# 64-bit weights narrowed to float32 by instructions on 1024 columns instead of 512

## The chip, the cores and the metric

The kernel runs on one core of a Trainium2 chip. The metric is the device time of one execution in microseconds. The engines are PE (matrix products; PEld is its weight load), DVE (vector), ACT (activation), POOL (GpSimd) and SP, which here only starts transfers. Each engine works through its own instructions in a fixed order and waits on semaphores that the others raise.

## The reference

Memory attention feeds a gated layer, whose output feeds eight experts, of which each token uses two:

```python
a = exp(phi - max(phi, axis=seq)); a = a / sum(a, axis=seq)          # 4 x 8 heads, 576 tokens, 32 slots
k_m, v_m = einsum(a, k), einsum(a, v)
attn = softmax(0.125 * q @ k_m.T) ;  x = attn @ v_m                  # x: 2304 x 512
h = x @ moe_w_in ;  x = (h * sigmoid(h)) @ moe_w_out                 # 512 x 2048, 2048 x 512
top2 of (x @ w_gate + log1p(exp(x @ w_noise)) * noise), softmax over the two
out[tokens of e] += weight * (relu(x @ w1[e]) @ w2[e])               # 8 experts, 512 x 1024 x 512
```

`moe_w_in` and `moe_w_out` are arrays of 64-bit floats, so the kernel sees each of their elements as two 32-bit integers, the low word and the high word.

## The kernel before

The span falls into four batches of attention and gated layer and then the experts. All products are made of float32 values split into a high part and a low part (`hi`, `lo`, each rounded for PE), so that three products stand for one.

**The gated layer.** A batch has 16 blocks `f` of 128 hidden columns and two token pieces `i` (256 and 320 tokens), which makes 32 steps `s`. Step `s` calls `mlp_h` (six products into the PSUM tile `h`, of which there are two; ACT makes `th`, DVE multiplies it, ACT and DVE or POOL split it into `gh` and `gl`), and three steps later `mlp_x` multiplies `gh`, `gl` by `woh[f]` and `wol[f]` (L299 to L301), into four PSUM tiles that stay open over the batch. A table of hooks (`at(step, function, ...)`) puts everything else at a step. A scheduler then fixes each engine's order.

**The weights.** In batch 0 alone the 64-bit weights are narrowed to float32 on the way. `moe_w_in` comes in eight parts of 256 columns (1 MB each, loaded as two halves of 512 element pairs a partition), is narrowed into `wi` (L237 to L238), is stored to `win_d` for the later batches, and is multiplied into the attention's values by `project` (L146), whose output is split into `wph`, `wpl`. `moe_w_out` comes in sixteen parts of 512 KB, one for each `f`. Narrowing one part of 512 columns is: ACT scales the low word to three bits (`lw`, L200), ACT scales the high word (L201), DVE shifts and joins them (L206); then for `w_in` DVE writes the sign (L210), and for `w_out` ACT takes the sign (`cg`, L216), POOL multiplies by it (L221), ACT makes `woh` (L264), and DVE (even `f`) or POOL (odd `f`) makes `wol` (L265). The loads go into the tag `st`, four buffers of 4 KB a partition; later the same buffers hold small tiles of the routing (`xs`, `xt`, `lt`, `z`, `xa`, `w1s`).

**The start.** The first instructions are written by hand after the loads: the softmax of batch 0 in two token pieces, `project(0, 1)`, the first `mlp_h`, then `narrow_wout(0)`, `narrow_win(1)` and `project(1, 1)` at step 2.

## Time and profile before

| what | us |
|---|---|
| median of three runs (lowest, highest) | 895.47 (894.5, 896.85) |
| the profiled execution, its own time | 896.81 |
| its span, first to last instruction | 895.0 |
| PE busy in the span | 847.6 (95%) |
| DVE, ACT, POOL busy in the span | 474.2, 359.2, 230.8 |
| PE busy in the first 45 us | 25.0 |

The span is what the profile covers; 1.8 us of the execution lie around it. Busy time of PE counts matmuls whose ends are modelled and which overlap, so it says where PE has work and not how fast it does it. An idle stretch is put down to what ended it.

### The profile page before, as it was taken

What the parts mean: (1) busy time and instruction counts of PE and PEld (TensorE: products, weight loads), DVE (VectorE), ACT (ScalarE), POOL (GpSimd) and SP (SyncE); (2) the same over time, 40 slices, a digit from 0 to 9 for tenths busy, and PEclk for the clock granted to TensorE, in tenths of its full rate; (3) what the DMA queues carried; (4) which work ended last, traced back from release to release, by engine and by line L of the source; (5) the groups of instructions that cost most, each with busy time, mean ns of one, the idle gap of its engine ahead of it and who ended that gap; (6) DMA issues with size and microseconds to landing.
All of it is one profiled execution on the core that took longest, in us unless ns stands there. A gap on an engine that the chain in (4) does not pass through costs nothing. (4 is left out here: it accounts for less than half of the span.)

```text
span 895.0 us, 14479 instructions
## 1 busy us (share of the span) xinstructions
PE 847.6 (95%) x5524; PEld 711.0 (79%) x5524; DVE 474.2 (53%) x1133; ACT 359.2 (40%) x836; POOL 230.8 (26%) x231
## 2 busy tenths in 40 slices
PE   4699899999999899999899999999999999999995
PEld 2367577788787787887889989989889798897983
DVE  3898995785277556554635444334444344343411
ACT  2689875444234354452214333324333133231400
POOL 0244340002000400310453234034342443322311
PEclk8599999999999999999999999999999999999998
DMA  9899842533201146221446455254552655424311
GB/s 306 273 323 330 267 154 94 168 130 65 86 5 48 48 158 243 57 75 49 106 145 197 151 167 170 62 177 135 149 144 72 188 148 158 132 80 138 88 26 38
DMA packets 76054, 124.14 MB, mean 139 GB/s; under 512 B 27715, under 2 KB 39363, under 8 KB 75975
## 3 DMA queue, kind: packets, MB, share of 16 engines
q1 hardware_dynamic: 46199, 90.66, 31.5%
q0 software_dynamic: 29776, 32.46, 12.7%
q8 instruction: 45, 0.74, 0.4%
q14 instruction: 34, 0.28, 0.1%
HBM read 99.69 MB, written 23.81 MB: 138 GB/s over the span
## 5 line engine op out<-in xcount | busy, mean ns | idle before, releaser
L597 PE MATMUL x<-w,gh 128*128 128x512 f32 (+5 forms) x640 | 202.5, 397 | 0.0
L597 PEld LDWEIGHTS x<-w,gh 128*128 128x128 f32 (+5 forms) x640 | 114.3, 183 | 27.5
L597 PE MATMUL x<-w,gl 128*128 128x512 f32 (+5 forms) x320 | 125.7, 393 | 0.0
L581 PE MATMUL x<-xh,w 128*128 128x290 f32 (+7 forms) x512 | 119.5, 306 | 0.0
L581 PE MATMUL h<-xh,w 128*128 128x290 f32 (+7 forms) x512 | 118.0, 303 | 1.0 <-issue 1.0
L277 PE MATMUL h<-ah,wph 128*128 128x320 f32 (+1 forms) x512 | 112.0, 303 | 2.5 <-DVE th L282 1.3
L299 PE MATMUL x<-woh,gh 128*128 128x512 f32 x256 | 106.7, 419 | 0.4 <-ACT woh L264 0.2
L277 PEld LDWEIGHTS h<-ah,wph 128*128 128x128 f32 x512 | 89.9, 192 | 19.0 <-DVE th L282 4.3
L300 PE MATMUL x<-wol,gh 128*128 128x512 f32 x256 | 102.3, 400 | 1.9 <-POOL wol L265 1.9
L301 PE MATMUL x<-woh,gl 128*128 128x512 f32 x256 | 101.5, 397 | 0.8 <-DVE gl L286 0.7
L444 POOL DMA_INDIRECT tab_d<-rows,slot x36 | 35.6, 988 | 240.3 <-DVE slot L441 192.2
L581 PEld LDWEIGHTS x<-xh,w 128*128 128x128 f32 x512 | 88.4, 190 | 0.0
L581 PEld LDWEIGHTS h<-xh,w 128*128 128x128 f32 x512 | 87.3, 189 | 1.0 <-issue 0.6
L282 DVE SCALAR_TENSOR_TENSOR th<-th,h 128x256 f32<-128x256 f32 (+1 forms) x128 | 57.6, 450 | 56.1 <-ACT th L280 43.2
L280 ACT ACTIVATE th<-h 128x256 f32<-128x256 f32 (+1 forms) x128 | 52.1, 407 | 82.9 <-PE h L277 66.6
L607 DVE SCALAR_TENSOR_TENSOR y<-x,tab,ex 116x512 f32<-116x512 f32 (+5 forms) x35 | 26.3, 750 | 109.6 <-PE x L597 105.3
L543 POOL DMA_INDIRECT xg<-x_d,gid x37 | 46.4, 1255 | 145.3 <-PE aux L563 76.6
L581 PE MATMUL h<-xl,w 128*128 128x290 f32 (+7 forms) x256 | 77.6, 303 | 1.1 <-issue 1.1
L581 PE MATMUL x<-xl,w 128*128 128x290 f32 (+7 forms) x256 | 78.6, 307 | 0.0
L277 PE MATMUL h<-ah,wpl 128*128 128x256 f32 (+1 forms) x256 | 76.4, 298 | 0.0
L285 ACT ACTIVATE gh<-th 128x256 fp32r<-128x256 f32 x128 | 53.2, 416 | 53.9 <-DVE th L282 49.3
L610 POOL DMA_INDIRECT out<-y,tab x40 | 51.7, 1292 | 87.6 <-DVE y L607 81.0
(167 smaller groups left out, 1391.8 us busy)
## 6 DMA issues: line engine op xcount, KB each, us to landing
w1s<-moe_w SPq DMA_DIRECT2D x32, 512.0 KB
w2s<-moe_w SPq DMA_DIRECT2D x32, 512.0 KB
wi<-win_d SPq DMA_DIRECT2D x24, 512.0 KB
kv<-kv SPq DMA_DIRECT2D x16, 650.0 KB
st<-moe_w_in SPq DMA_DIRECT2D x16, 512.0 KB
st<-moe_w_out SPq DMA_DIRECT2D x16, 512.0 KB
q<-qt SPq DMA_DIRECT2D x16, 288.0 KB
out<-z SPq DMA_DIRECT2D x1, 4608.0 KB
```

What stands on the lines that cost most here:

```text
L277: pe.matmul(p[:, :w], wt[:, g, c:c + 128], AH[b, g][at][:, t0:t0 + w], start=(n == 0), stop=(n == 5))
L280: act.activation(th[:, :w], p[:, :w], AF.Tanh, scale=0.5)
L282: dve.scalar_tensor_tensor(u[:, :w], th[:, :w], 1.0, p[:, :w], op0=OP.add, op1=OP.mult)
L285: act.activation(gh, u[:, :256], AF.Copy)
L299: pe.matmul(X2[j], gh[:, r], woh[f], start=(f == 0), stop=False)
L300: pe.matmul(X2[j], gh[:, r], wol[f], start=False, stop=False)
L301: pe.matmul(X2[j], gl[:, r], woh[f], start=False, stop=(f == NF - 1))
L444: st = pool.indirect_dma_start(out=tab_d, out_offset=bass.IndirectOffsetOnAxis(ap=slot[:, j, k:k + 1], axis=0), in_=rows.bitcast(I32)[:, j ...
L543: last = pool.indirect_dma_start(out=XG[k, j], out_offset=None, in_=x2_d if k else x2_d[:KNOWN, :], in_offset=bass.IndirectOffsetOnAxis(ap ...
L581: pe.matmul(p[:, :w], wt[:, d, c], x[:, d, r], start=(n == 0), stop=(n == 11))
L597: mm = pe.matmul(p, g[:, r], w[:, f, :], start=(n == 0), stop=(n == 23))
L610: st = pool.indirect_dma_start(out=a["out"], out_offset=bass.IndirectOffsetOnAxis(ap=TAB[k][:, j, 0:1], axis=0), in_=y, in_offset=None, bo ...
```

## The change

Three things change in the code. The low words are written back in place, into the loaded buffer, so the tile `lw` is gone. The loads go into a pool of their own with three buffers of 8 KB a partition, each filled by two loads (`raw`), and all of the narrowing but that of part 0 of `w_in` and of parts 0 and 1 of `w_out` is done by instructions on 1024 columns: a part of `w_in` at once, and the parts of `w_out` in pairs, fetched at step 2f-6 and narrowed at step 2f-2. A pair has one `wo` tile (before: two tiles in turn, one part each), and POOL makes the low parts of every second pair, DVE those of the others. At step 32 the pool is closed and a pool with the tag `st` (four buffers) is opened in its place for the routing's small tiles. [...]

```diff
-    def stage(src):
-        t = m1.tile([128, 512, 2], I32, name="st", tag="st", bufs=4)
-        sp.dma_start(t.rearrange("p a w -> p (a w)").rearrange("p (c x) -> p c x", c=src.shape[1]), src)
+    def stage(src, x=0, t=None):
+        t = t or s0.tile([128, 1024, 2], I32, name="raw", bufs=3)
+        v = t[:, 512 * x:512 * (x + 1), :].rearrange("p a w -> p (a w)")
+        sp.dma_start(v.rearrange("p (c x) -> p c x", c=src.shape[1]), src)
         return t
 
     def shrink(t, m):
-        low = ap_.tile([128, 512], I32, name="lw", bufs=1)
-        act.activation(low, t[:, :, 0].bitcast(U32), AF.Identity, scale=LOW, bias=lowb)
+        low = t[:, :, 0]
+        act.activation(low, low.bitcast(U32), AF.Identity, scale=LOW, bias=lowb)
...
-            g = ap_.tile([128, 512], BF16, name="cg", bufs=1)
+            g = ap_.tile([128, 1024], BF16, name="cg", bufs=1)[:, :t.shape[1]]
...
-        for g, t in enumerate(ST.pop(("i", i))):
-            narrow(t, WI[i][:, 2 * g:2 * g + 2, :].rearrange("p r f -> p (r f)"), True)
+        narrow(ST.pop(("i", i)), WI[i].rearrange("p r f -> p (r f)"), True)
...
-    def narrow_wout(i):
-        w = ap_.tile([128, DM], F32, name="wo", bufs=2)
-        narrow(ST.pop(("o", i)), w)
-        act.activation(woh[i], w, AF.Copy)
-        (pool if i % 2 else dve).tensor_sub(wol[i], w, woh[i].bitcast(F32))
+    def narrow_wout(i, n=2):
+        t = ST["o", i // 2]
+        r = slice(i % 2 * DM, (i % 2 + n) * DM)
+        hi, lo = (x[i // 2][:, r] for x in wop)
+        w = ap_.tile([128, 2 * DM], F32, name="wo", bufs=1)[:, :n * DM]
+        narrow(t[:, r, :], w)
+        act.activation(hi, w, AF.Copy)
+        (pool if i // 2 % 2 else dve).tensor_sub(lo, w, hi.bitcast(F32))
...
-    for f in range(1, NF):
-        at(max(0, 2 * f - 5), fetch_wout, f)
-        at(2 * f - 1, narrow_wout, f)
+    at(0, fetch_wout, 1)
+    at(1, narrow_wout, 1, 1)
+    for f in range(2, NF, 2):
+        for x in range(2):
+            at(max(0, 2 * f - 6), fetch_wout, f + x)
+        at(2 * f - 2, narrow_wout, f)
...
+    at(32, open_s1)
...
-    nc = bacc.Bacc("TRN2", target_bir_lowering=False, num_devices=1)
+    nc = bacc.Bacc("TRN2", target_bir_lowering=False, num_devices=1,
+                   dynamic_dma_scratch_size=8192)
```

The orders of the engines differ in batch 0 alone; from PE's instruction 336 on (of some 4370 rows) they are the same. Three places follow.

**The first narrowings, on ACT and DVE.** These are ACT's instructions from the first narrowing of `w_out` (`wo`, `cg`, `woh`) to the first `th`, before:

```order
L200 ACTIVATE lw<-st,lowb 128x512
L201 ACTIVATE wo<-st 128x512
L216 ACTIVATE cg<-st 128x512
L201 ACTIVATE wi<-st 128x512
L200 ACTIVATE lw<-st,lowb 128x512
L264 ACTIVATE woh_89<-wo 128x512
L201 ACTIVATE wi<-st 128x512
L163 ACTIVATE sct<-sct 128x2x320
L200 ACTIVATE lw<-st,lowb 128x512
L280 ACTIVATE th<-h 128x256
```

And the same stretch in the change:

```order
L204 ACTIVATE raw<-raw,lowb 128x512
L205 ACTIVATE wo<-raw 128x512
L220 ACTIVATE cg<-raw 128x512
L204 ACTIVATE raw<-raw,lowb 128x1024
L271 ACTIVATE woh_92<-wo 128x512
L166 ACTIVATE sct<-sct 128x2x320
L205 ACTIVATE wi<-raw 128x1024
L287 ACTIVATE th<-h 128x256
```

The copy of the high words of `w_in` part 1 stood half before and half behind `woh`; now it stands as a whole behind `woh` and the softmax's exponential (L163, now L166). DVE's rows there, from the softmax's second token piece (`smx` is its maximum, `ssm` its sum) to the sign of `w_in` part 1, are these in the change:

```order
L164 TENSOR_REDUCE smx<-sct 128x2x10
L210 SCALAR_TENSOR_TENSOR wo<-wo,raw 128x512
L165 TENSOR_TENSOR sct<-sct,smx 128x2x320
L272 TENSOR_TENSOR wol_100<-wo,woh_92 128x512
L173 TENSOR_REDUCE ssm<-sct 128x2x10
L174 TENSOR_SCALAR ssm<-ssm 128x2x10
L210 SCALAR_TENSOR_TENSOR wi<-wi,raw 128x1024
L175 RECIPROCAL ssm<-ssm 128x2x10
L214 SCALAR_TENSOR_TENSOR wi<-raw,wi 128x1024
L180 STREAM_TRANSPOSE att<-sct 128x320 x2
```

Before, the join of `wo` (L206) stood ahead of the reduction, and the join and sign of `w_in` part 1 stood as two of 512 columns each, one pair before the reciprocal and one around it.

**The first waits of PE.** These are PE's instructions from `project(1, 1)` (`aux<-wi,kvt`) on, before; `ah` are the attention's split outputs:

```order
L146 MATMUL aux<-wi,kvt 32x256 x8
L299 MATMUL x_442<-woh_89,gh 128x512
L300 MATMUL x_442<-wol_105,gh 128x512
L277 MATMUL h<-ah_287,wph 128x320
L277 MATMUL h<-ah_287,wph 128x256
L277 MATMUL h<-ah_288,wph 128x256
L277 MATMUL h<-ah_287,wpl 128x256
```

In the change one product of the eight stands at that place, twelve `h` products follow, and then come the other seven; the last of the twelve and what follows are:

```order
L284 MATMUL h<-ah_275,wph 128x320
L284 MATMUL h<-ah_274,wpl 128x320
L149 MATMUL aux<-wi,kvt 32x256 x7
L306 MATMUL x_419<-woh_92,gh 128x512
L307 MATMUL x_419<-wol_100,gh 128x512
L308 MATMUL x_419<-woh_92,gl 128x512
```

So PE still meets the narrowed `w_in` part 1 before any of these `h` products, and finishes `project(1, 1)` behind them.

**The first pair, on POOL.** POOL's work on `w_out` parts 1 to 3 before (L239 stores `wi`, L286 makes `gl`):

```order
L221 TENSOR_TENSOR wo<-wo,cg 128x512
L265 TENSOR_TENSOR wol_106<-wo,woh_90 128x512
L221 TENSOR_TENSOR wo<-wo,cg 128x512
L286 TENSOR_TENSOR gl<-th,gh 128x256
L239 DMA win_d<-wi 128x1024
```

And in the change, where `wol_101` is the low part of the pair 2 and 3:

```order
L225 TENSOR_TENSOR wo<-wo,cg 128x512
L225 TENSOR_TENSOR wo<-wo,cg 128x1024
L272 TENSOR_TENSOR wol_101<-wo,woh_93 128x1024
L293 TENSOR_TENSOR gl<-th,gh 128x256
L243 DMA win_d<-wi 128x1024
```

POOL made the low part of part 1 and left that of part 2 to DVE; now it makes those of 2 and 3 in one instruction of twice the columns.

## Rows read from the trace of the kernel before

**Rows 1.** Stretches of the span: us, PE, PEld, DVE, ACT, POOL busy, clock, DMA share, GB/s.

```profile
25.00:45.00 20.00, 13.35 (x75) 7.30 (x76) 17.72 (x37) 15.05 (x32) 5.25 (x6) 0.60 0.84 264
45.00:90.00 45.00, 41.47 (x325) 31.01 (x324) 40.57 (x82) 40.86 (x93) 20.27 (x19) 1.00 0.97 327
90.00:135.00 45.00, 40.50 (x276) 29.88 (x275) 41.22 (x74) 35.10 (x82) 18.12 (x16) 1.00 0.62 205
135.00:860.00 725.00, 716.56 (x4640) 618.83 (x4639) 360.24 (x913) 260.92 (x619) 178.64 (x159) 1.00 0.39 119
```

**Rows 2.** What PE waited for, 25 to 45 us: total, times, longest.

```profile
PE aux L146 <- DVE ssm L171: 5.0, 1, 5.0
```

**Rows 3.** What PE waited for, 45 to 135 us.

```profile
PE x L300 <- POOL wol L265: 1.9, 3, 0.8
...
PE aux L146 <- DVE wpl L253: 1.7, 1, 1.7
```

**Rows 4.** What ACT waited for, 45 to 135 us.

```profile
ACT woh L264 <- POOL wo L221: 5.6, 8, 1.2
...
ACT wo L201 <- DMA st<-moe_w_out: 0.9, 1, 0.9
```

**Rows 5.** ACT groups by shape, 25 to 135 us: busy, mean ns, idle before.

```profile
L200 ACT ACTIVATE lw<-st,lowb 128x512 int32<-128x512 uint32 x30 | 22.9, 764 | 1.0 <-DVE wi L206 0.7 <-DVE wo L206 0.3
...
L264 ACT ACTIVATE woh<-wo 128x512 fp32r<-128x512 f32 x16 | 10.1, 632 | 6.0 <-POOL wo L221 6.0
...
L163 ACT ACTIVATE sct<-sct 128x1152 f32<-128x1152 f32 x1 | 1.2, 1170 | 0.0
```

**Rows 6.** DVE groups by shape, 25 to 135 us.

```profile
L265 DVE TENSOR_TENSOR wol<-wo,woh 128x512 fp32r<-128x512 f32 x8 | 5.5, 685 | 0.7 <-ACT woh L264 0.6
...
L162 DVE TENSOR_TENSOR sct<-sct,smx 128x1152 f32<-128x1152 f32 x1 | 1.4, 1351 | 0.0
```

**Rows 7.** POOL groups by shape, 25 to 135 us.

```profile
L221 POOL TENSOR_TENSOR wo<-wo,cg 128x512 f32<-128x512 f32 x16 | 19.4, 1214 | 16.3 <-DVE wo L206 8.6 <-DVE rs L127 2.5 <-ACT gc L293 1.5
...
L265 POOL TENSOR_TENSOR wol<-wo,woh 128x512 fp32r<-128x512 f32 x8 | 10.7, 1340 | 8.8 <-ACT woh L264 8.8
```

**Rows 8.** ACT timeline, 28.5 to 34 us: start, us, instruction, idle before.

```profile
29.36 0.75 ACT L200 ACTIVATE lw<-st,lowb 128x512 int32<-128x512 uint32 x1
30.01 0.66 ACT L201 ACTIVATE wo<-st 128x512 f32<-128x512 f32 x1
30.57 0.66 ACT L216 ACTIVATE cg<-st 128x512 bf16<-128x512 f32 x1
...
32.75 0.63 ACT L264 ACTIVATE woh<-wo 128x512 fp32r<-128x512 f32 x1 [0.32 <-POOL wo L221]
```

**Rows 9.** PE timeline, 36 to 41.6 us.

```profile
36.16 1.08 PE L146 MATMUL aux<-wi,kvt 64*32 64x256 f32 x8 [4.96 <-DVE ssm L171]
...
39.65 1.06 PE L277 MATMUL h<-ah,wph 128*128 128x320 f32 x3
```

**Rows 10.** DVE and POOL timelines, 31 to 38.6 us.

```profile
31.32 0.81 DVE L161 TENSOR_REDUCE smx<-sct 128x20 f32<-128x640 f32 x1
...
32.16 1.23 DVE L162 TENSOR_TENSOR sct<-sct,smx 128x640 f32<-128x640 f32 x1
...
31.56 1.16 POOL L221 TENSOR_TENSOR wo<-wo,cg 128x512 f32<-128x512 f32 x1 [5.60 <-DVE wo L206]
...
37.10 1.44 POOL L173 TENSOR_TENSOR sct<-sct,ssm 128x640 f32<-128x640 f32 x1 [4.39 <-issue]
```

**Rows 11.** DVE and POOL timelines, 47 to 49 and 118 to 121 us.

```profile
47.15 1.28 POOL L265 TENSOR_TENSOR wol<-wo,woh 128x512 fp32r<-128x512 f32 x1 [0.74 <-ACT woh L264]
...
47.41 1.31 DVE L286 TENSOR_TENSOR gl<-th,gh 128x256 fp32r<-128x256 f32 x1
...
118.73 0.75 DVE L185 TENSOR_TENSOR ah<-att,ah 128x576 fp32r<-128x576 f32 x1
...
118.95 1.55 POOL L221 TENSOR_TENSOR wo<-wo,cg 128x512 f32<-128x512 f32 x1 [0.69 <-DVE wo L206]
```

## The prediction

> **What bounds the kernel now.** I read the table of stretches first, since an average over the span would hide that the change lives in batch 0 alone. From 135 to 860 us PE is busy 716.6 of 725 us at the full granted clock [rows 1], and the engines' orders there are the same in both programs, so nothing is to be had or lost there. From 45 to 135 us, where the narrowing runs, PE is idle 90 - 41.5 - 40.5 = 8.0 us, while ACT is busy 40.9 of 45 us and then 35.1, and DVE 40.6 and 41.2: three engines are close to full, PE most of all. [...]

> Then the waits of PE. The longest single one is 5.0 us, before `project(1, 1)` [rows 2]; the row names `ssm`, but the instruction that the matmul needs is the sign of the first half of `w_in` part 1 (L210), which DVE writes just before it. In 45 to 135 us the largest are 1.9 us for `wol` made by POOL and 1.7 us for `wpl` [rows 3]. ACT stands 5.6 us in front of `woh`, waiting for POOL's product, and 0.9 us in all for a load of `w_out` [rows 4]. So the loads are not late, though the transfer engines are 97% busy from 45 to 90 us [rows 1]; deeper staging has little to cure. What counts is when three things come: the first sign, `woh` and `wol`.

> **The change part by part.**

> *Fewer instructions.* ACT has 96 narrowing instructions and keeps 54, DVE 56 and 32, POOL 24 and 13. On ACT 640 more columns take 1.170 - 0.632 = 0.538 us [rows 5], 0.84 ns a column or 0.43 us for 512; back to back, one of 512 columns costs 30.57 - 30.01 = 0.56 us and a `lw` 30.01 - 29.36 = 0.65 us [rows 8]. So merging two copies saves 0.13 us and two `lw` 0.22 us (nothing, if the low words' own price is all by column): 28 x 0.13 + 14 x 0.22 = 6.7 us, with 3.6 us as the lower end. On DVE 640 columns take 1.351 - 0.685 = 0.666 us, 1.04 ns a column or 0.53 for 512, so at most 0.15 us is saved on each of 24, 3.6 us, and less back to back [rows 6]. These are upper bounds for the span, as PE waits only 8.0 us in all there; it gains only where a late `th`, `gh` or `woh` is what it waits for.

> [...]

> Instructions of 1024 columns do not stand in the trace. ACT: 0.63 + 0.43 = 1.06 us, `lw` 0.76 + 0.43 = 1.19 us. DVE: 0.69 + 0.53 = 1.22 us. POOL: between 1.2 (as for 512) and 2.4 us for the sign's product, between 1.3 and 2.7 us for `wol` [rows 7]; a product of 640 columns took 1.44 us against 1.16 us [rows 10], in proportion to its columns, so I take 2.2 and 2.4 us. The strided write of the low words has no row; I count it as free, at worst 0.1 us on each of 18.

> *The first narrowings.* [...] At 47.41 us DVE's `gl` took 1.31 us and ended as POOL's `wol` let go, and at 118.95 us POOL's product took 1.55 us, since DVE's subtraction had begun 0.22 us earlier [rows 11]. Now follow the change. The join of `wo` comes behind the reduction, which ended at 32.13 us [rows 10] and now starts some 0.9 us earlier; the join ends near 31.8 us. DVE goes straight on to its subtraction of 640 columns (0.15 + 640 x 1.04 ns = 0.82 us), to 32.6 us, and POOL's product, which ran first before (31.56 to 32.72 us, with DVE's subtraction stretched to 1.23 us [rows 10]), now waits for it: 33.6 us. ACT's `woh` starts there, not at 32.75 [rows 8]; behind it stand the exponential (0.63 us) and the copy of 1024 columns, which ends at 35.9 us. Join and sign of 1024 columns take to 38.4 us, and PE's `project(1, 1)` starts at 38.5 us, not at 36.16 [rows 9]. POOL's product of the softmax, at 37.10 before, is kept out by that sign and ends near 39.6 us, not 38.54 [rows 10]. The transposes and splits behind it release the `h` products at about 40.7 us, not 39.65 [rows 9]. Seven eighths of `project(1, 1)` (some 1.9 us at the lower clock, by the 1.08 us of a half [rows 9]) now come after these, and the `h` products themselves wait for `ah`, which stands behind another join of 1024 columns on DVE. Where `h` of steps 1 and 2, the project and the first `x` are all done, PE is 3 to 4 us later. Some of that comes back within a few steps, because ACT and DVE used the time; I keep 2.5 us, with 1 and 4 as ends.

> *The first pair.* A part of 512 columns went through ACT, DVE, POOL, ACT and POOL in 0.65 + 0.56 + 0.56 + 0.69 + 1.21 + 0.63 + 1.34 = 5.6 us [rows 5 to 8]. A pair takes 1.1 + 1.0 + 1.0 + 1.2 + 2.2 + 1.1 + 2.4 = 10.0 us, and nothing of it can be used before all of it is there. Its order on ACT puts the low words and the high words of `w_in` part 3 (2.1 us) ahead of `woh`. The first pair starts on ACT near 46 us, so POOL is done at 58 us or later; `x` of step 4 would want it near 55 us (it started at 52.9 us before, and PE is 2.5 us late). That is a wait of 3 us, ends 0.5 and 5. The later POOL pairs (6 and 7, 10 and 11, 14 and 15) begin five steps ahead, 13 us or so, and may be late by 0 to 1 us each; I take 1.5 us for the three.

> *What comes back.* While PE waits, ACT and DVE catch up, so the 8.0 us of old waits shrink; with 3.6 to 6.7 us less work on ACT I take 3 us.

> *No price.* Loads issued earlier: they were waited for 0.9 us [rows 4]. The pool opened at step 32: its first tile comes a step after the last narrowing's, whose buffers are long read. [...]

> *Sum.* 2.5 + 3.0 + 1.5 - 3.0 = +4.0 us on the profiled execution's own 896.8 us (span 895.0), so 900.8; that execution lies 1.3 us above the median shown, and against the median it is 895.5 + 4.0 = **899.5 us**. Its own range is 897 to 903 us.

> **The rivals.**

> *Faster.* ACT is the second limit, and its 3.6 to 6.7 us reach PE. For it: ACT is busy 91% from 45 to 90 us, and PE's waits for `wpl` and `wol` go back to it. Against it: PE itself is busy 92% there, and at the start ACT idles, it does not work. If the scheduler's new order also kept the first `wol` in time, 5 us would come off: 890.5 us. The point that decides is PE's idle time from 45 to 135 us: under 4 us, this is it.

> *No change.* The late start is all given back by step 32, because ACT and DVE run ahead while PE waits: 895.5 us. For it: PE has only 8 us of idle time there to begin with and any lag turns into slack for the others. Against it: work of PE that is late stays late, unless old waits vanish.

> *Much slower: POOL's long instructions hold DVE.* Eleven POOL instructions of 2.2 to 2.4 us take the place of 22 of about 1.25. A DVE instruction that meets one waits up to its end, twice as long as the 0.9 us of 47.41 [rows 11]; `th` stands behind it on DVE, and with two `h` tiles PE has about a step, 2.5 us, of cover. DVE is busy 41.2 of 45 us from 90 us on [rows 1], so it can't take 11 x 0.7 us more without PE standing: +8 us, 903.5 us. [...]

> **How the numbers follow.** A run of this kernel can be told from no change at about 0.3%, 2.7 us. Chances: my forecast 0.42, of which 0.05 falls within 0.3%; much slower 0.18; no change 0.17; faster 0.23, of which 0.03 falls within. So faster 0.20, same 0.25, slower 0.55. Faster and slower both hold much, so the range is 891 to 906 us, leaving out about one in ten on either side; the forecast's own is 897 to 903.

> **What would show it.** Right: `project(1, 1)` starts after 38 us; `woh` of part 0 near 33.6; PE waits for `wol` of the first pair 2 us or more; ACT's narrowing of 1024 columns near 1.06 and 1.19 us; DVE instructions of 2 us beside POOL's. Wrong: `project(1, 1)` at 36 us again, or PE's idle time from 45 to 135 us well under 8 us, or any growth behind 135 us. What could make it wrong is the order in which DVE and POOL get to their instructions near 32 us, on which 0.9 us and all that follows hang, and the old waits vanishing faster than I count.

## The result and the profile after

| | median us | ratio to before, 95% interval |
|---|---|---|
| before, six executions | 895.88 (894.5 to 896.85) | |
| changed, six executions | 902.59 (900.37 to 905.15) | 1.0076 (1.0058 to 1.0093) |
| changed again, five executions, another chip | 893.67 (892.55 to 895.63) | 1.0083 (1.0070 to 1.0097) |

The changed kernel is slower by 6.7 us; the forecast was 4.0 us, 899.5. The profiled execution of the changed kernel took 904.81 us (span 903.0), one of its two longest. The chip of the second set is about 1% quicker for both kernels (886.83 us for the kernel before), so from here on kernels of different sets are compared by ratio, and one "us" of a ratio difference means that difference times 887 us.

The stretches of the changed kernel, with the columns of [rows 1]:

```profile
25.00:45.00 20.00, 9.86 (x58) 5.27 (x58) 15.95 (x29) 12.45 (x22) 6.40 (x6) 1.00 0.85 278
45.00:90.00 45.00, 39.03 (x297) 29.57 (x284) 38.09 (x62) 36.99 (x68) 18.27 (x14) 0.92 0.82 275
90.00:135.00 45.00, 40.63 (x285) 30.05 (x284) 41.82 (x63) 31.50 (x63) 17.29 (x11) 0.96 0.65 227
135.00:860.00 725.00, 717.54 (x4641) 617.58 (x4640) 365.59 (x925) 265.28 (x630) 179.91 (x160) 1.00 0.40 120
```

PE's idle time grew from 6.7 to 10.1 us in the first row and from 3.5 to 6.0 in the second; behind 135 us it did not grow. ACT is busy 3.9 and 3.6 us less, and PE has nothing of it. A second thing was in none of the prediction's cases: the granted clock is 0.92 and 0.96 where it was 1.00.

What PE waited for, first 25 to 45 us, then 45 to 135 us (where before had [rows 2] and [rows 3]):

```profile
PE aux L149 <- DVE wi L214: 8.6, 2, 6.9
...
PE h L284 <- DVE th L289: 3.6, 3, 1.3
PE aux L141 <- DVE wpl L257: 1.8, 1, 1.8
PE x L308 <- POOL gl L293: 1.5, 2, 1.2
PE x L308 <- DVE gl L293: 1.2, 3, 0.5
PE x L307 <- POOL wol L272: 1.1, 1, 1.1
```

The start, on PE, DVE, POOL and ACT, where before had [rows 9, 10]:

```profile
38.49 1.03 PE L149 MATMUL aux<-wi,kvt 64*32 64x256 f32 x2 [6.90 <-DVE wi L214]
40.56 1.06 PE L284 MATMUL h<-ah,wph 128*128 128x320 f32 x3 [1.04 <-ACT ah L187]
...
31.68 0.82 DVE L165 TENSOR_TENSOR sct<-sct,smx 128x640 f32<-128x640 f32 x1
...
31.93 1.58 POOL L225 TENSOR_TENSOR wo<-wo,cg 128x512 f32<-128x512 f32 x1 [5.98 <-DVE wo L210]
...
33.54 0.63 ACT L271 ACTIVATE woh<-wo 128x512 fp32r<-128x512 f32 x1 [1.20 <-POOL wo L225]
```

Each step of the forecast walk stands there: DVE's subtraction first, POOL's product ending at 33.51, `woh` at 33.54, `project(1, 1)` at 38.49, `h` at 40.56. The prices of 1024 columns were right too, in the groups by shape from 25 to 135 us (as [rows 5 to 7]):

```profile
L204 ACT ACTIVATE raw<-raw,lowb 128x1024 int32<-128x1024 uint32 x14 | 17.3, 1238 | 0.0
L225 POOL TENSOR_TENSOR wo<-wo,cg 128x1024 f32<-128x1024 f32 x7 | 15.7, 2246 | 12.8 <-DVE wo L210 10.2 <-ACT cg L220 2.7
L272 POOL TENSOR_TENSOR wol<-wo,woh 128x1024 fp32r<-128x1024 f32 x4 | 9.8, 2438 | 5.5 <-ACT woh L271 5.5
L271 ACT ACTIVATE woh<-wo 128x1024 fp32r<-128x1024 f32 x7 | 7.4, 1056 | 6.2 <-POOL wo L225 6.2
L272 DVE TENSOR_TENSOR wol<-wo,woh 128x1024 fp32r<-128x1024 f32 x3 | 3.7, 1221 | 0.0
```

The first pair, on DVE, POOL and PE from 52 to 61 us:

```profile
52.83 2.17 DVE L301 TENSOR_TENSOR gc<-th,gc 128x64 fp32r<-128x64 f32 x1
54.91 0.41 DVE L289 SCALAR_TENSOR_TENSOR th<-th,h 128x256 f32<-128x256 f32 x1
55.24 1.21 DVE L210 SCALAR_TENSOR_TENSOR wi<-wi,raw 128x1024 int32<-128x1024 int32 x1
56.49 3.28 DVE L214 SCALAR_TENSOR_TENSOR wi<-raw,wi 128x1024 int32<-128x1024 int32 x1
...
52.72 2.19 POOL L225 TENSOR_TENSOR wo<-wo,cg 128x1024 f32<-128x1024 f32 x1 [6.34 <-DVE wo L210]
56.08 2.61 POOL L272 TENSOR_TENSOR wol<-wo,woh 128x1024 fp32r<-128x1024 f32 x1 [1.17 <-ACT woh L271]
58.65 1.71 POOL L293 TENSOR_TENSOR gl<-th,gh 128x256 fp32r<-128x256 f32 x1
...
55.38 0.50 PE L284 MATMUL h<-ah,wph 128*128 128x256 f32 x2 [1.33 <-DVE th L289]
58.74 0.50 PE L307 MATMUL x<-wol,gh 128*128 128x512 f32 x1 [1.14 <-POOL wol L272]
60.41 0.79 PE L308 MATMUL x<-woh,gl 128*128 128x512 f32 x1 [1.17 <-POOL gl L293]
```

Read it from the bottom. PE stops three times, 3.6 us in all. Once for `wol`, as forecast. Once for a `gl` that POOL makes and that stands behind `wol` in POOL's order. And once for `th`, a DVE instruction of 0.41 us: in front of it DVE's `gc`, 64 columns, took 2.17 us and ended 0.09 us after POOL's product, which had begun 0.11 us earlier. This is the hold of [rows 11], now twice as long: `gc` took 0.22 us at 48.09 with POOL idle, so the hold is 1.95 us, where it was 0.9 us (`gl` 1.31 us at 47.41, 0.43 us at 54.90). The next one is worse: the sign of `wi` took 3.28 us, over POOL's `wol`, and 1.23 us at 96.62 with POOL idle. It goes the other way too: POOL's `gl` began 1.1 us before that sign ended and took 1.71 us, where it took 0.73 us at 100.31.

This is not the only place. Beside ten of POOL's eleven instructions on 1024 columns in this profile a DVE instruction takes between 1.50 and 3.28 us. PE stands for a second one as well, since `wpl` comes behind `gc` and a `th` on DVE:

```profile
89.80 2.25 POOL L225 TENSOR_TENSOR wo<-wo,cg 128x1024 f32<-128x1024 f32 x1 [1.17 <-DVE wo L210]
89.98 2.15 DVE L301 TENSOR_TENSOR gc<-th,gc 128x64 fp32r<-128x64 f32 x1
92.86 0.44 PE L141 MATMUL aux<-ident,src 128*128 128x128 f32 x2 [1.84 <-DVE wpl L257]
```

That wait was 0.9 us in the kernel before.

Then the clock. PE's windows of the changed kernel, and the same windows of its second profile (903.0 and 890.8 us long):

```profile
59.00:67.00 8.00, 6.83 (x22) 5.72 (x22) 4.20 (x9) 5.84 (x9) 4.05 (x3) 0.57 0.72 230
93.00:98.00 5.00, 5.00 (x21) 4.35 (x21) 4.71 (x7) 4.42 (x10) 0.00 (x0) 0.66 0.98 357
```

```profile
59.00:67.00 8.00, 7.04 (x39) 5.88 (x39) 6.47 (x15) 6.58 (x13) 3.40 (x3) 1.00 0.84 271
93.00:98.00 5.00, 5.00 (x54) 3.65 (x52) 4.56 (x10) 4.99 (x10) 2.37 (x3) 1.00 0.71 187
```

Behind the three pauses the granted clock of the first profile is 0.50 from 60 to 66 us (0.57 over the window), and again from 94 to 97 us behind that pause of 1.8 us (0.66 over its window). PE gets 22 matmuls done in 8 us instead of 39. The second profile has the same program and the same pauses (1.4, 1.2 and 1.2 us), and its clock stays at 1.00 in both windows.

### The profile page after: what moved, and what is told of

Read it like the earlier page. It is cut to its first block, busy times and chain, and to the rows that moved or that the text cites. A ratio compares the mean times of both kernels' runs of the same rounds, so it can differ in the third digit from the quotient of the medians.

```text
span 903.0 us, 14383 instructions
## 1 busy us (share of the span) xinstructions
PE 850.8 (94%) x5524; PEld 713.9 (79%) x5524; DVE 477.5 (53%) x1109; ACT 354.9 (39%) x794; POOL 230.4 (26%) x220
## 4 chain that ended last, share of the span: by engine, by line
PE 79%; DVE 8%; issue 3%; ACT 2%; DMA 2%; POOL 1%; POOLq 0%; ACTq 0%; DVEq 0%
PE x L604 25%; PE x L588 12%; PE h L588 12%; PE h L284 8%; PE x L306 6%; PE x L308 5%; PE x L307 5%; PE aux L570 2%; PE aux L149 2%; DVE gl L293 1%; DVE th L289 1%; PE aux L345 1%; PE aux L338 1%; DVE wpl L257 1%; DMA q<-qt 1%
## 5 line engine op out<-in xcount | busy, mean ns | idle before, releaser
L284 PE MATMUL h<-ah,wpl 128*128 128x320 f32 (+1 forms) x256 | 77.4, 302 | 0.0
L293 DVE TENSOR_TENSOR gl<-th,gh 128x256 fp32r<-128x256 f32 x120 | 58.5, 488 | 31.2 <-ACT gh L292 26.0
```

The lines of the kernel that those rows point to most:

```text
L284: pe.matmul(p[:, :w], wt[:, g, c:c + 128], AH[b, g][at][:, t0:t0 + w], start=(n == 0), stop=(n == 5))
L293: (pool if b == 0 and (2 * f + i) % 4 == 0 else dve).tensor_sub(gl, u[:, :256], gh.bitcast(F32))
```

## The experiments

Theory A was that the width of the instructions causes the loss; rival B that the storage does. After the first four runs A was divided: the start (A as in my sum) against the pairs of `w_out` (C); then a pair's latency (L) against POOL's keeping DVE out (H). Twelve kernels ran, each in five rounds against the kernel before.

**The kernel again.**

> The changed kernel once more. Theory A: part of its loss is that PE pauses for 1 to 1.5 us at a time between 52 and 61 us and near 92 us, after which the granted clock falls to 0.5 for 6.6 and 3.3 us; that costs up to 4.9 us and need not happen in each execution. Then the single times spread from 900 to 905 us and go with the mean granted clock of the span (about 900.5 at 0.995, 905 at 0.988), and a profile of higher mean clock shows matmuls of 512 columns at 0.40 us throughout from 48 us on. Rival: the clock makes no difference to the time (the low stretches fall where PE waits anyway); then times at 0.988 and 0.995 do not differ by over 1 us.

893.67 us, 1.0083. The six executions of the first set go with the mean granted clock of the span: 900.37 at 0.995, 900.77 and 902.53 at 0.994, 902.65 at 0.991, 904.81 at 0.989, 905.15 at 0.988. The five of this set lie at 0.994 to 0.997 and from 892.55 to 895.63 us. (Only executions of this kernel can be ordered so: the profiled execution of the kernel before has 0.979 at 896.81 us, within 1 us of its median; its clock is low at the start, 0.60 from 25 to 45 us [rows 1], see the last section.) If I match the products with `wol` of the two profiles one by one, the second gains 2.8 us between 58.7 and 67.3 us and 1.5 us between 93.8 and 97.4, just where the first ran at the lower clock (0.57 and 0.66 above), and 0.9 us before that; some 0.8 us are given back by 108 us. ACT's `th` of step 5, ahead of the falls, lies 0.65 us apart in the two profiles, that of step 31, the last of batch 0, 4.24 us (142.70 and 138.46). So the falls cost the first profile some 3.6 us, and they need not happen. A loss of some 4.5 to 6 us is left without them (first set: fastest execution 900.37 against 895.88 or, fastest against fastest, 894.5).

**The descriptor space alone.** The kernel before with this one setting:

```diff
-    nc = bacc.Bacc("TRN2", target_bir_lowering=False, num_devices=1)
+    nc = bacc.Bacc("TRN2", target_bir_lowering=False, num_devices=1,
+                   dynamic_dma_scratch_size=8192)
```

> The kernel before with the descriptor space of 8192 bytes and nothing else; every engine's order is that of before. Theory A (the loss is the width of the narrowing instructions): 895.5 us, within 1.5 us of before. Rival B (the loss is in the storage: descriptor space, buffers, pool): slower by 2 us or more, with the growth behind 135 us, where the indirect transfers are.

1.0001 (0.9992 to 1.0010): nothing.

**All of the storage, none of the width.** In the changed kernel:

```diff
-        narrow(ST.pop(("i", i)), WI[i].rearrange("p r f -> p (r f)"), True)
+        for g in range(2):
+            narrow(t[:, 512 * g:512 * (g + 1), :], w[:, 512 * g:512 * (g + 1)], True)
...
-        at(2 * f - 2, narrow_wout, f)
+            at(2 * (f + x) - 1, narrow_wout, f + x, 1)
```

> The changed kernel with its storage (three double buffers, low words in place, pool opened at step 32, descriptor space 8192), but all narrowing by instructions on 512 columns and the parts of w_out one by one as before. Theory A: 895 us, 893 to 898; project(1, 1) starts near 36.2 us, no DVE instruction is held over 1.5 us. Rival B: 902 us as in the changed kernel.

0.9995 (0.9986 to 1.0004). Rival B falls: double buffers, low words in place, the pool opened at step 32 and the descriptor space of 8192 together cost nothing and gain nothing. The width, with the pairing of the parts that goes with it, is the cause.

**Part 1 of `w_in` in halves.** The `narrow` of part 1 alone is cut as in the diff above.

> The changed kernel with part 1 of w_in narrowed in two halves of 512 columns as before, everything else as changed. Theory A (my sum: the late start is carried to the end): project(1, 1) starts near 36.3 us and 2 to 3 us come off, a ratio of 1.0055. Rival C (the start is given back within two steps; the loss arises at the pairs of w_out from step 4 on): project(1, 1) starts near 36.3 us all the same, but the ratio stays at 1.007 to 1.009.

1.0088 (1.0070 to 1.0106): no gain. `project(1, 1)` starts at 36.82 us (38.26 in the second profile of the changed kernel), but the `h` products behind it start at 40.31 us against 40.33, and the first pair has not moved; its rows on POOL, and a `gl` on DVE:

```profile
52.21 2.14 POOL L225 TENSOR_TENSOR wo<-wo,cg 128x1024 f32<-128x1024 f32 x1 [4.84 <-DVE wo L210]
55.52 2.37 POOL L275 TENSOR_TENSOR wol<-wo,woh 128x1024 fp32r<-128x1024 f32 x1 [1.17 <-ACT woh L274]
57.84 0.91 POOL L296 TENSOR_TENSOR gl<-th,gh 128x256 fp32r<-128x256 f32 x1
...
55.78 2.39 DVE L296 TENSOR_TENSOR gl<-th,gh 128x256 fp32r<-128x256 f32 x1 [0.96 <-ACT gh L295]
```

In the second profile of the changed kernel `wol` began at 55.43. PE is busy 6.28 us from 50 to 60 us, no more than there (6.31), but waits for other things: 1.0 us for a `th`, 1.3 us for ACT's `gh`, which stands behind `woh`, and 1.5 us for the `gl` above, which took 2.39 us beside POOL's `wol` (0.42 us at 50.06 in the changed kernel, with POOL idle). The clock also fell in this profile (0.91 from 50 to 60 us; equal products of 512 columns 0.43 us apart from 58.8 to 61.4 us and 0.23 us apart at 63), so not all of its loss is that of the pairs.

**`w_out` part by part, `w_in` on 1024 columns.** The second half of the diff of the storage run.

> The changed kernel with w_in narrowed by 1024 columns, but w_out part by part on 512 columns at the old steps. Rival C: nearly all of the loss goes, ratio 1.001 (0.999 to 1.003), with project(1, 1) still at 38.5 us. Theory A: the start's 2.5 us stay, ratio 1.003 to 1.004.

1.0013 (1.0002 to 1.0024), with the start as late as in the changed kernel (38.5 us).

**`w_in` in halves, `w_out` in pairs.** The first half of that diff.

> The changed kernel with w_in narrowed in halves of 512 columns everywhere, but w_out in pairs on 1024. Rival C: the loss stays, ratio 1.007, with DVE still held for 2 us and more by POOL. Theory A: the start's part goes, ratio 1.004 to 1.005.

1.0084 (1.0067 to 1.0102): all of the loss, with a start as before. These two runs are the plainest of the study: the loss is in the pairs, some 6 us, and 1.2 us go with the wide `w_in`. The profile is of this run's slowest execution and has falls of the clock (0.92 from 45 to 90 us and from 90 to 135), so some of what the start gave back may have gone into them.

**The first pair alone undone.**

```diff
+        if f == 2:
+            at(3, narrow_wout, 2, 1)
+            at(5, narrow_wout, 3, 1)
+        else:
+            at(2 * f - 2, narrow_wout, f)
```

> The changed kernel with the first pair alone (parts 2 and 3 of w_out) narrowed singly at steps 3 and 5, as before. If the first pair is the main loss, as in my sum (3 us of it): ratio 1.004, and PE does not pause for wol of part 2 near 58 us. If each of POOL's four pairs costs about the same: ratio 1.006 to 1.007.

1.0046 (1.0031 to 1.0062). By the medians the first pair is 0.0037 or 3.3 us of the loss, and the six other pairs are 1.0046 - 1.0013, 2.9 us, each give or take some 2 us. PE's busy time from 50 to 60 us shows the first in one column; these are the rows of the second profile of the changed kernel, of `w_in` on 1024 columns alone, and of the first pair undone:

```profile
50.00:60.00 10.00, 6.31 (x43) 4.23 (x43) 9.50 (x10) 7.43 (x14) 6.76 (x4) 1.00 0.70 233
```

```profile
50.00:60.00 10.00, 9.93 (x65) 7.73 (x63) 7.90 (x11) 9.35 (x21) 4.20 (x4) 1.00 0.79 263
```

```profile
50.00:60.00 10.00, 10.00 (x66) 7.93 (x64) 8.26 (x12) 9.34 (x20) 4.45 (x4) 1.00 0.84 279
```

PE does 43 matmuls there with the pair and 65 or 66 without; before, it was busy 9.40 us.

But the profiles do not show these 3 us as a loss that lasts. This is where ACT's `th` of a step starts, in us (steps counted from 0; the chips of these runs differ by 0.3%, 886.83 and 889.17 us for the kernel before):

| profile of | step 1 | step 8 | step 9 | step 31 |
|---|---|---|---|---|
| before, smaller descriptor space | 42.78 | 61.30 | 66.34 | 134.00 |
| `w_in` wide, `w_out` part by part | 44.58 | 63.26 | 68.47 | 136.07 |
| `w_in` in halves, `w_out` in pairs | 42.73 | 61.99 | 68.25 | 144.11, clock fell |
| first pair undone | 44.93 | 63.49 | 68.93 | 138.53 |
| changed, second profile | 44.34 | 66.50 | 68.54 | 138.46 |

Undoing the first pair gains 3.0 us at step 8, undoing the start and the wide `w_in` 4.5 us, and at step 9 all of it is gone. ACT's order has `woh` of the second pair (or of part 4) there, behind POOL's product, then high words of `w_in`, an exponential and this `th`; that this queue is the next fixed point is read from the rows, not tested. From step 9 to 31 the lag behind the first line grows by 2 us with the later pairs and not at all without pairs. And where no pair follows, the late start does stay: 1.8 us at step 1, 2.1 at step 31.

**POOL's instructions in halves.** All other engines keep their order, so this run takes the length of POOL's instructions alone.

```diff
-            pool.tensor_mul(m, m, g)
+            for x in range(0, t.shape[1], 512):
+                r = slice(x, x + 512)
+                pool.tensor_mul(m[:, r], m[:, r], g[:, r])
```

(The low part on POOL is cut in the same way.)

> The changed kernel with POOL's product and POOL's low parts each cut into two instructions of 512 columns; the orders of PE, ACT and DVE are those of the changed kernel. Theory A: between two POOL instructions DVE gets its turn, so the DVE instructions of 2.17 us (at 52.8) and 3.28 us (at 56.5) fall to about 1.3 and 2.0 us, th comes 1 to 2 us earlier, PE pauses less and the clock falls less: 899 us, 897 to 901. The start stays: project(1, 1) near 38.5 us. Rival (only the latency of a pair counts, not the holding of DVE): no change from the changed kernel, 902.5 us, since the halves together take as long on POOL.

1.0073 (1.0059 to 1.0086). In the trace it does what H says:

```profile
52.98 1.19 DVE L308 TENSOR_TENSOR gc<-th,gc 128x64 fp32r<-128x64 f32 x1
54.09 0.41 DVE L296 SCALAR_TENSOR_TENSOR th<-th,h 128x256 f32<-128x256 f32 x1
54.67 1.62 DVE L210 SCALAR_TENSOR_TENSOR wi<-wi,raw 128x1024 int32<-128x1024 int32 x1 [0.17 <-ACT wi L205]
56.33 1.23 DVE L214 SCALAR_TENSOR_TENSOR wi<-raw,wi 128x1024 int32<-128x1024 int32 x1
```

`gc` takes 1.19 and the sign 1.23 us, and from 50 to 61 us the wait for `th` is gone, while those for `wol` and `gl` stay:

```profile
PE x L314 <- POOL wol L277: 1.3, 1, 1.3
PE x L315 <- POOL gl L300: 1.1, 1, 1.1
```

So one of the three pauses belongs to the hold of `gc`. The other two are POOL's queue, but not free of the hold: between the halves of `wol` DVE's sign now gets in, and the two halves take 3.55 us where the whole took 2.61:

```profile
56.38 3.55 POOL L277 TENSOR_TENSOR wol<-wo,woh 128x512 fp32r<-128x512 f32 x2 [1.17 <-ACT woh L273]
```

The whole kernel gains 0.9 us by the medians, within the intervals, where theory A had 3.5. In this profile PE's products of 320 columns went from 0.47 to 0.30 us at 49.4 us, in that of the changed kernel of the same set PE's rise came at 44.3, which may have eaten some of the rest: `th` is 1.0 us later here at step 3 and level at step 31 (138.47). That is argued, not shown.

**Latency.** Three runs were to tell L from H: the end of the chain in halves (POOL's product, `woh` and the low part), the pairs hooked one step earlier, and one step later; a fourth joined the first two. The halves at the end of the chain (POOL's product as above), and the step earlier (a step later has 2f - 5 and 2f - 1):

```diff
-        act.activation(hi, w, AF.Copy)
-        (pool if i // 2 % 2 else dve).tensor_sub(lo, w, hi.bitcast(F32))
+        for x in range(0, n * DM, DM):
+            q = slice(x, x + DM)
+            act.activation(hi[:, q], w[:, q], AF.Copy)
+            (pool if i // 2 % 2 else dve).tensor_sub(lo[:, q], w[:, q], hi[:, q].bitcast(F32))
...
-            at(max(0, 2 * f - 6), fetch_wout, f + x)
-        at(2 * f - 2, narrow_wout, f)
+            at(max(0, 2 * f - 7), fetch_wout, f + x)
+        at(2 * f - 3, narrow_wout, f)
```

> The changed kernel with the end of a pair's chain in two halves of 512 columns: POOL's product, ACT's woh and the low part, so that the first part of a pair is ready some 2.3 us before the second; scaling, copy, sign and join stay on 1024. Theory L (a pair costs by its latency, because nothing of it can be used before all of it is there): ratio 1.004 to 1.005, and the waits for wol and for what stands behind it near 57 to 61 us go. Rival H (a pair costs by the time that POOL's instructions keep DVE out, which halves of POOL alone hardly changed): ratio 1.007, as with POOL's halves alone.

> The changed kernel with the fetch and the narrowing of each pair hooked one step (some 2.5 us) earlier. Theory L: each pair that was late is less late; ratio 1.004 to 1.005. Rival H: the same instructions meet DVE as often; ratio 1.008.

> The changed kernel with the fetch and the narrowing of each pair hooked one step later: the suspected cost made larger. Theory L: the seven pairs are later by up to a step each where they were already on the edge, ratio 1.012 or more, with PE's waits for woh and wol growing. Rival H: ratio 1.008.

> The changed kernel with both: halves at the end of a pair's chain and the pairs hooked one step earlier. Theory L: most of the pairs' cost is gone, ratio 1.001 to 1.003; whether the fewer ACT instructions then make it faster than before (0.998) is the open question. Rival H: ratio 1.006 to 1.007.

1.0051 (1.0038 to 1.0064), 1.0049 (1.0036 to 1.0062), 1.0043 (1.0031 to 1.0056) and 1.0047 (1.0031 to 1.0064): all four gain about 3 us, the one that was to cost more included, and the two cures do not add up. Simple L falls, and plain H (no change) with it. The traces say why hooking earlier and later told nothing of the first pair: the scheduler left it where it was. POOL's first wide `wol`, hooked a step earlier and a step later:

```profile
55.84 2.61 POOL L272 TENSOR_TENSOR wol<-wo,woh 128x1024 fp32r<-128x1024 f32 x1 [1.17 <-ACT woh L271]
```

```profile
56.20 2.64 POOL L272 TENSOR_TENSOR wol<-wo,woh 128x1024 fp32r<-128x1024 f32 x1 [1.17 <-ACT woh L271]
```

What they changed is the order around the pairs. By how much each of these orders suits PE better, and through which neighbour, stays open: `th` of step 31 stands at 137.19 to 139.32 us in the four profiles, on both sides of the 138.46 of the changed kernel's second profile, with falls of the clock in three of the four (0.92, 0.94 and 0.94 from 45 to 90 us) and none in that one (1.00). Since orders that leave the first pair in place gain as much as the run that undid it, its 3.3 us can't be put down to that pair alone. No version beat the kernel before; the storage with instructions of 512 columns equals it.

## Why the prediction was right, and where its sum was wrong

**Direction, place and prices: right.** The forecast's own range was 897 to 903 us, and the median 902.59 lies at its upper end. The walk to `project(1, 1)` was right within 0.02 us (38.5 against 38.49), `h` within 0.2 us, the widths' prices within 0.08 us, and the first pair's `wol` ended at 58.7 us where I had 58 or later.

**The start, 2.5 us: wrong in the sum.** The step that failed is "work of PE that is late stays late" as I used it to add 2.5 us to the delays of the pairs. With the pairs in place, undoing the start gave nothing (1.0088 and 1.0084 against 1.0083), since ACT, DVE and POOL came to the next steps as late as ever and PE's lead ran out in front of them: 4.5 us at step 8, 0.3 at step 9. Without pairs, start and wide `w_in` together left 1.2 us (0.2 to 2.1). A delay upstream of a later wait that does not depend on it must not be added to that wait.

**The first pair, 3.0 us: near in size, incomplete in kind.** PE's pauses there are 3.6 us, and undoing the pair gave 3.3 us by the medians; but in the profiles the gain is gone a step later, so the size may be luck. And I had put all of it on `wol`, with a wait of 2 us or more as a sign; that is 1.1 us, and the rest is POOL's `gl` queued behind (1.2 us) and the `th` held back on DVE (1.3 us). The last is the mechanism of my rival "POOL's long instructions hold DVE". It was no separate case: it happened together with the forecast, beside ten of POOL's eleven wide instructions, and PE stood directly for at least two of the holds. The rival's price of 8 us was too high. The trace shows the hold at the new length: 64 columns took 2.17 us next to a product of 2.19 us, and 1.19 us next to halves. It does not show it for every DVE instruction: in the changed kernel two `phi` took 0.87 us from 77.17 us, beside the product of 77.42, and 0.89 us from 68.23 us with POOL idle.

**The later pairs, 1.5 us: too small.** All pairs but the first measured 2.9 us by the medians, some 2 us in the profiles.

**What comes back, 3.0 us: not seen.** ACT worked 7.5 us less from 45 to 135 us, and the old waits did not shrink: PE idled 10.3 us there instead of 8.0. The saving itself was well priced: on ACT a scaling of 1024 columns starts 1.14 us ahead of the next instruction (35.99 to 37.13) and a copy 1.02 us (37.13 to 38.15), 0.16 and 0.10 us less than two of 512 [rows 8]. My estimates were 0.22 and 0.13.

**The clock: missing.** None of my cases had a fall of PE's clock behind the new pauses. In the first profile it cost some 3.6 us, and over all executions the spread from 900.4 to 905.2 us goes with it. That the sum of 4.0 us lies near the loss without falls (4.5 to 6 us) is partly luck: the start was too high, the later pairs too low, and nothing came back.

## What to carry to other kernels

Fewer, wider instructions saved 0.16 and 0.10 us a merger on ACT here, and PE's waits did not shrink; the first chain from POOL's product to the end of `wol` grew from 3.2 us (45.26 to 48.43) to 6.0 us (52.72 to 58.69). So ask what the first consumer needs, and what each wide instruction holds up on its own engine and, as here on DVE and POOL, on the other (up to 2.0 us). An instruction undone may gain 3 us at one step and nothing at the next, so follow its gain beyond the wait that it removes. Of several delays in a row, price only those that the next fixed point does not swallow: undo them one by one. And behind pauses of 3.6 us on PE the granted clock was 0.50 for 6 us in one profile, and behind 3.8 us it stayed at 1.00 in another, so judge by several executions and look at the clock of each.

## What the runs showed of the hardware that was not expected

**The same pauses, with and without a fall of the clock.** PE was busy 6.78 of 10 us from 50 to 60 us in one profile of the changed kernel and 6.31 in the other. In the first the granted clock from 59 to 67 us was 0.57, in the second 1.00.

```profile
46.00:49.00 3.00, 3.00 (x9) 2.43 (x8) 2.26 (x6) 2.15 (x7) 1.17 (x2) 1.00 0.98 349
```

```profile
46.51 0.63 PE L308 MATMUL x<-woh,gl 128*128 128x512 f32 x1
46.94 0.63 PE L306 MATMUL x<-woh,gh 128*128 128x512 f32 x1
...
49.75 0.39 PE L307 MATMUL x<-wol,gh 128*128 128x512 f32 x1
49.98 0.40 PE L308 MATMUL x<-woh,gl 128*128 128x512 f32 x1
```

The product at 46.51 holds PE for 0.43 us, the one at 49.75 for 0.23 us. The moment of that rise was 41.1 us in the profile of before, 46.1 and 44.3 us in the two of the changed kernel, and 49.4 us in that of POOL's halves. Here the spacing of equal products (0.43 and 0.23 us) tells the speed, and the clock's column (1.00 from 45 to 50 and from 50 to 60 us) does not.
